# Half of the first MLP matmul moved beside the attention of the last two token groups, in an adaLN block on one core

## Chip, cores, metric

The kernel runs on one core of a Trainium2 chip. The metric is the device time of one execution in microseconds (us), as the median of several runs.

## The reference

The block works on x of 2048 tokens by 512 features, with modulation vectors from a small conditioning vector c, sliding-window attention and a token-mixing MLP.

```python
mod = (_silu(c) @ w_mod).reshape(c.shape[0], 6, 1, -1)
sa, ca, ga, sb, cb, gb = ...
h = _layernorm(x) * (1 + ca) + sa
x = x + ga * _A_ref(h, A_wqkv, A_wo)       # 32 heads of 16, window of 256 keys, causal
h = _layernorm(x) * (1 + cb) + sb
x = x + gb * _B_ref(h, ...)                # mixes over tokens:
#   h = layernorm(x)                                      (2048, 512)
#   u = gelu(einsum('bsd,sf->bdf', h, w1) + b1)           w1: (2048, 1792)
#   y = einsum('bdf,fs->bds', u, w2) + b2                 w2: (1792, 2048)
```

The contraction of the first MLP matmul runs over all 2048 tokens. Its result can be finished only when the last token's attention is done, but the part of the sum over the early tokens can be formed before.

## The kernel before, in words

Tokens are held as 16 tiles of 128 (xres, names x_65 to x_80 in the trace). Attention works on four groups G of 512 tokens, each in four units of eight heads (g8), each unit in five steps (four in group 0) that take one row of CHUNKS. A step has three parts: the score matmuls (emit_scores, L390) into two PSUM tiles of the pool ps_s, the exponential and the masks (emit_exp_mask, ScalarE L404, VectorE L411 and L416), and the matmuls with V and with ones (emit_av, L435). The scores of step i+1 are written ahead of the values of step i-1, so that ScalarE has work; ps_s has two buffers and a step needs both. After a unit emit_norm divides (L446 to L448).

Beside the steps of group G a list bg of background jobs is worked off at an even rate (per_step, L513): proj_work(G+1), which is the layer norm, transposes (L269), and Q, K, V projections (L285, L294, L313) of the next group, and post_work(G-1), which is the output projection of the group before (L344), its residual (L348), and two layer norms (L350 to L367) that end in the tiles hb (hb_81 to hb_96), the operand of the MLP. K is copied (L299) and then spread by GpSimd into a zero-padded form (L301). The padded V tiles are zeroed by three GpSimd memsets at the start (L452). Within what the code order and the buffers allow, a scheduler of the framework sets the final order on each engine.

After group 3 stands post_work(3) alone (L531), then the first MLP matmul. It takes 16 token tiles (sc) times 14 column blocks (fc) of w1, 224 matmuls of 128 by 512. Six column blocks accumulate side by side (L562), the other eight follow one by one (L570). The first half of w1, w1a, is loaded during group 1, the second half, w1b, and w2 (L539, L543) only when the attention's pools are released (att.close, L533), all on SyncE's (SP) queue. The GELU (L554) reads PSUM, VectorE scales (L557), and the second MLP matmul (L578, 224 matmuls) writes output tiles that VectorE finishes (L583, L588).

All first loads are on SP's queue as well, in the order c, x of group 0, w_mod, w_qkv, the rest. The first exponential needs x, its layer norm (xn, L245), the modulation (ps_fm L188, modFM L194), the transposes, Q and K.

## Time and profile before

| quantity | value |
|---|---|
| time, median of 3 runs (lowest to highest) | 326.96 us (326.34 to 328.46) |
| time of the profiled execution | 324.87 us |
| its span from first to last instruction | 323.2 us |
| outside the span | 1.67 us |
| TensorE (PE) matmul busy | 274.4 us, 85% |
| VectorE (DVE) busy | 209.4 us, 65% |
| ScalarE (ACT) busy | 182.3 us, 56% |
| GpSimd (POOL) busy | 39.2 us, 12% |

Busy times are sums of instruction durations over the span. Matmuls are pipelined, so that a matmul's duration is longer than the distance between two of them, and PE's busy share is above its real load. The stages of this kernel have different limits, so that shares over the span say little; the windows below cut it into stages. The granted TensorE clock is given as a share of full speed.

### The profile page before, as it was taken

How to read it: one execution, taken by the hardware profiler on the slowest of the kernel's cores; microseconds unless marked ns; L12 is line 12 of the kernel's file. 1: busy time of each engine (PE TensorE's matmuls, PEld its weight loads, DVE VectorE, ACT ScalarE, POOL GpSimd, SP SyncE). 2: the span in 40 equal slices, each digit the busy share in tenths (PEclk: the TensorE clock that was granted, in tenths of full speed). 3: DMA queues.
4: the chain of work that ended last, by engine and by line, in shares of the span. 5: the costliest groups of instructions: out<-in, count | busy, mean ns of one | idle time of the engine just before them, and what ended most of it. 6: DMA issues, size and time to landing. Idle time of an engine off the chain costs nothing.

```text
span 323.2 us, 7621 instructions
## 1 busy us (share of the span) xinstructions
PE 274.4 (85%) x3277; PEld 133.9 (41%) x3313; DVE 209.4 (65%) x487; ACT 182.3 (56%) x241; POOL 39.2 (12%) x57
## 2 busy tenths in 40 slices
PE   0388988989897889998888878968999999999994
PEld 0343435544454344454344443423334444444441
DVE  6889997758989847889846787369403112445443
ACT  2005789899996999988999999930007111000000
POOL 9632302230100230010050000000000000000000
PEclk9999999999998999979999997679999999999998
DMA  6994039000000000000000000000399910111110
GB/s 205 350 210 148 2 106 350 5 3 2 3 2 0 2 2 2 2 3 2 3 2 2 2 2 2 2 1 2 116 380 411 408 50 0 51 45 38 49 49 34
DMA packets 18121, 24.61 MB, mean 76 GB/s; under 512 B 5032, under 2 KB 14248, under 8 KB 18088
## 3 DMA queue, kind: packets, MB, share of 16 engines
q1 hardware_dynamic: 18088, 24.13, 21.7%
q8 instruction: 26, 0.43, 0.6%
q14 instruction: 7, 0.06, 0.1%
HBM read 22.03 MB, written 2.10 MB: 75 GB/s over the span
## 4 chain that ended last, share of the span: by engine, by line
PE 43%; DVE 24%; ACT 23%; issue 6%; DMA 2%; SPq 0%
ACT et L404 17%; PE py L578 15%; PE pu L570 8%; PE pss L390 5%; DVE st L237 4%; PE pox L435 3%; DVE VT_147 L323 3%; DVE xn L245 3%; PE pu L562 2%; PE pv L313 2%; PE pa L344 2%; ACT lz L446 2%; PE poy L435 2%; ACT lz L447 2%; DMA w1b<-in_B_w_dram 2%
## 5 line engine op out<-in xcount | busy, mean ns | idle before, releaser
L404 ACT ACTIVATE et<-pss 128x1024 bf16<-128x1024 f32 (+1 forms) x152 | 147.0, 1024 | 21.6 <-PE pss L390 20.8
L435 PE MATMUL poy<-et,ones_bd 128*32 128x128 bf16 (+4 forms) x768 | 43.1, 263 | 0.2
L411 DVE TENSOR_TENSOR et<-et,maskt 128x256 bf16<-128x256 bf16 (+2 forms) x104 | 33.4, 344 | 12.1 <-ACT et L404 11.8
L578 PEld LDWEIGHTS <-w2r 128*128 128x128 bf16 x224 | 21.9, 98 | 26.4
L416 DVE TENSOR_TENSOR et<-et,maskt 128x512 bf16<-128x512 bf16 x48 | 20.5, 427 | 13.5 <-ACT et L404 12.7
L435 PE MATMUL pox<-et,VT_147 128*32 128x320 bf16 (+4 forms) x352 | 20.2, 263 | 3.7 <-DVE OT_1_155 L448 1.5
L435 PEld LDWEIGHTS <-ones_bd 128*32 128x32 bf16 x768 | 19.6, 99 | 7.1 <-issue 3.6
L554 ACT ACTIVATE g<-pu,b1FM 128x512 bf16<-128x512 f32 x14 | 8.9, 696 | 16.2 <-PE pu L570 16.2
L240 ACT ACTIVATE rs<-mv,eps_t 128x4 f32<-128x4 f32 x12 | 3.6, 298 | 20.4 <-DVE mv L238 20.3
L435 PEld LDWEIGHTS <-VT_147 128*32 128x32 bf16 x352 | 9.1, 96 | 13.8 <-issue 12.9
L299 DVE CAST kb<-pk 128x512 bf16<-128x512 f32 x16 | 11.0, 687 | 4.8 <-PE pk L294 4.7
L435 PE MATMUL pox<-et,VT_148 128*32 128x320 bf16 (+4 forms) x208 | 11.0, 261 | 1.1 <-DVE OT_1_151 L448 0.6
L323 DVE CAST VT_147<-pv 64x512 bf16<-64x512 f32 x16 | 11.0, 689 | 0.8 <-PE pv L313 0.5
L435 PE MATMUL pox<-et,VT_149 128*32 128x320 bf16 (+4 forms) x208 | 11.2, 262 | 0.0
L557 DVE TENSOR_TENSOR guT_4330<-g,bc_gb 128x512 bf16<-128x512 bf16 x1 | 0.4, 424 | 16.1 <-ACT g L554 16.1
L313 PE MATMUL pv<-wqkv,h1T_159 128*64 128x256 bf16 x128 | 10.7, 294 | 0.0
L447 ACT ACTIVATE lz<-lz 128x512 f32<-128x512 f32 x16 | 10.5, 658 | 0.0
L446 ACT ACTIVATE lz<-poy 128x512 f32<-128x512 f32 x16 | 9.8, 613 | 1.1 <-PE poy L435 1.1
L294 PE MATMUL pk<-h1T_158,wqkv 128*128 128x512 bf16 x32 | 9.4, 410 | 0.7 <-DVE kb L299 0.6
L554 ACT ACT_TABLE_LOAD x1 | 1.3, 1283 | 15.5 <-PE pu L562 15.5
L285 PE MATMUL pq<-h1T_158,wqkv 128*128 128x512 bf16 x26 | 8.3, 408 | 1.6 <-issue 0.6
L570 PEld LDWEIGHTS <-w1b 128*128 128x128 bf16 x64 | 6.3, 98 | 7.6
(360 smaller groups left out, 574.7 us busy)
## 6 DMA issues: line engine op xcount, KB each, us to landing
w2r<-in_B_w_dram SPq DMA_DIRECT2D x14, 512.0 KB, 10.1
w1a<-in_B_w_dram SPq DMA_DIRECT2D x8, 448.0 KB, 7.9
...
```

What stands on the lines that cost most here:

```text
L237: nc.vector.bn_stats(out=st[:], in_=t[:])
L313: nc.tensor.matmul(pv[KB * par : KB * (par + 1), i, :].rearrange("p (a d) -> p a d", d=DH), lhsT=h1T[r2][:, dc, tok], rhs=wv[:, dc, par, : ...
L323: nc.vector.tensor_copy(out=dst, in_=src)
L390: nc.tensor.matmul(pss[:, jj, col : col + KB * nq], lhsT=KT[r][g8][rows, kbi, :, :], rhs=QT[G % 2][g8][rows, KB * qs : KB * (qs + nq)], st ...
L404: nc.scalar.activation(out=et[:, 2 * a : 2 * a + 2, lo:D], in_=tiles[a][:, :, lo:D], func=ACT.Exp, scale=SCORE_SCALE,)
L411: nc.vector.tensor_tensor(out=dst, in0=dst, in1=msk.to_broadcast([P, 4, KB * mn]), op=ALU.mult,)
L416: nc.vector.tensor_tensor(out=dst, in0=dst, in1=maskt[:, m0 : m0 + 2, :].unsqueeze(1).to_broadcast([P, 4, 2, KB]), op=ALU.mult,)
L435: nc.tensor.matmul(dst[32 * j : 32 * j + 32, KB * qs : KB * (qs + nq)], lhsT=VT[r][:, kbi, 4 * u.g8 + j, :] if isv else ones_bd[:], rhs=et ...
L446: nc.scalar.activation(out=lz[:], in_=u.y[:], func=ACT.Ln)
L447: nc.scalar.activation(out=lz[:], in_=lz[:], func=ACT.Exp, scale=-1.0)
L570: nc.tensor.matmul(pu[:], lhsT=w1s(sc, fc), rhs=hb[sc][:], start=(sc == 0), stop=(sc == NT - 1),)
L578: nc.tensor.matmul(py[:], lhsT=w2r[:, fc, tb * P : (tb + 1) * P], rhs=guT[fc][:], start=(fc == 0), stop=(fc == NF - 1),)
```

## The change

1. partial(fc) forms the sum over the first eight token tiles (1024 tokens) for one column block, eight matmuls into a ps_d buffer, and VectorE copies it to SBUF in fp32. Four of these jobs are appended to bg in group 2, ten in group 3. 112 of the 224 matmuls of the first MLP matmul thus stand among the attention steps.
2. w1 is loaded by pairs of column blocks, eight token tiles at a time (load_w1): the seven first halves at the start of group 1, each second half when the pair's two partials are formed.
3. After group 3 only the second eight token tiles are multiplied (mlp1), and before the GELU VectorE adds the partial sum. The PSUM pools stay those of the attention, so that tiles of two banks (kind s) hold two column blocks.
4. The loads of c and of the first two parts of w_mod go to ACT's queue, the w_qkv loads are split so that the columns of the first unit come first, and b1 and b2 come last.
5. V's first tile is zeroed by VectorE, the other two by 16 GpSimd memsets (zero_jobs), and group 0's first K tile is spread by VectorE straight from PSUM (no copy, no GpSimd).
6. Buffers: one h1T instead of two, h2 4 instead of 5, kb 2 instead of 3. Background jobs start a step later (credit) and are spread over one step less (nsteps - 2).

```diff
-    dma.dma_start(out=c4[:], in_=c.rearrange("o (j p) -> (o j) p", p=P))
+    nc.scalar.dma_start(out=c4[:], in_=c.rearrange("o (j p) -> (o j) p", p=P))
+    for v in (0, 1):
+        nc.scalar.dma_start(out=wmod[:, :, v * D : (v + 1) * D], in_=wm_v[:, :, v * D : (v + 1) * D])
     for t in range(4):
         dma.dma_start(out=xres[t][:], in_=x_dram[t * P : (t + 1) * P, :])
     for v in (0, 1):
-        dma.dma_start(out=wmod[:, :, v * D : (v + 1) * D], in_=wm_v[:, :, v * D : (v + 1) * D])
-    for v in (0, 1, 2):
-        dma.dma_start(out=wqkv[:, :, v * D : (v + 1) * D], in_=w_v[:, :, v * D : (v + 1) * D])
+        dma.dma_start(out=wqkv[:, :, v * D : v * D + P], in_=w_v[:, :, v * D : v * D + P])
+    dma.dma_start(out=wqkv[:, :, 2 * D : 3 * D], in_=w_v[:, :, 2 * D : 3 * D])
+    for v in (0, 1):
+        dma.dma_start(out=wqkv[:, :, v * D + P : (v + 1) * D], in_=w_v[:, :, v * D + P : (v + 1) * D])
...
+            if G == 0 and g8 == 0:
+                for par in range(2):
+                    nc.vector.tensor_scalar(
+                        out=KT[r3][g8][:, :, par, :], in0=pk[:].rearrange("p (b k) -> p b k", k=KB),
+                        scalar1=mask_par[:, par : par + 1], scalar2=0.0, op0=ALU.mult, op1=ALU.add,
+                    )
+                return
...
+    def load_w1(pair, half):
+        t = w1pool.tile([P, 8, 2 * P], BF, name=f"w1p{pair}", tag=f"w1p{pair}")
+        dma.dma_start(out=t[:], in_=w1_v[:, 8 * half : 8 * half + 8, 2 * P * pair : 2 * P * (pair + 1)])
+        w1t[pair, half] = t
...
+    def partial(fc):
+        pu = ps_d.tile([P, D], F32, name="pu", tag="psd")
+        for sc in range(8):
+            nc.tensor.matmul(
+                pu[:], lhsT=w1s(sc, fc), rhs=hb[sc][:], start=(sc == 0), stop=(sc == 7),
+            )
+        pool = partA if fc < 4 else partB
+        t = pool.tile([P, D], F32, name=f"part{fc}")
+        nc.vector.tensor_copy(out=t[:], in_=pu[:])
+        part[fc] = t
+        if fc % 2 == 1:
+            load_w1(fc // 2, 1)
...
-    for r in range(3):
-        nc.gpsimd.memset(VT[r][:], 0.0)
+    nc.vector.memset(VT[0][:], 0.0)
...
+    zero_jobs = [lambda r=r, kb=kb: zero_v(r, kb) for r in (1, 2) for kb in range(8)]
...
-            post = post_work(u.G - 1) if u.G > 0 else mod_jobs + [early, wod_scale]
+            post = post_work(u.G - 1) if u.G > 0 else mod_jobs + [early, wod_scale] + zero_jobs[8:]
...
+            if u.G == 0:
+                bg = zero_jobs[:8] + bg
+            if u.G == 2:
+                bg += [lambda fc=fc: partial(fc) for fc in range(4)]
+            if u.G == 3:
+                bg += [lambda fc=fc: partial(fc) for fc in range(4, NF)]
             nsteps = sum(1 for s in steps if s[0].G == u.G)
-            per_step = len(bg) / (nsteps - 1)
-            credit = 0.0
+            per_step = len(bg) / (nsteps - 2)
+            credit = -per_step
...
+    f_tiles([("s", [0, 1]), ("s", [2, 3]), ("x", [4]), ("y", [5])])
+    for w in pw:
         w()
+    mlp1(first, range(8, NT))
     att.close()
...
-    w1b = w2pool.tile([P, 8, F], BF, name="w1b")
-    for sc in range(8):
-        dma.dma_start(out=w1b[:, sc, :], in_=w1_v[:, 8 + sc, :])
...
+    def gelu(fc):
+        a = gtmp.tile([P, D], F32, name="a")
+        nc.vector.tensor_tensor(out=a[:], in0=ftiles[fc], in1=part[fc][:], op=ALU.add)
         g = gtmp.tile([P, D], BF, name="g")
         nc.scalar.activation(
-            out=g[:], in_=pu[:], func=ACT.Gelu_apprx_tanh, bias=b1FM[:, fc : fc + 1], scale=1.0,
+            out=g[:], in_=a[:], func=ACT.Gelu_apprx_tanh, bias=b1FM[:, fc : fc + 1], scale=1.0,
         )
```

The order on the engines changes at three places. On GpSimd, near the start, the kernel before zeroes the three V tiles (VT_147 to VT_149) between the identity and the masks:

```order
masks.py:197 MEMSET identity 128x128
L117 MEMSET ones_bd 128x32
L452 MEMSET VT_147 128x4096
masks.py:199 ISA
masks.py:199 AFFINE_SELECT identity<-identity 128x128
L118 MEMSET ones_bd 64x16
L119 MEMSET ones_bd 64x16
L452 MEMSET VT_148 128x4096
L452 MEMSET VT_149 128x4096
```

Now the masks come first, and the 16 short memsets of two V tiles (VT_144, VT_145) follow in one run ahead of the K tiles:

```order
L234 COPY maskt<-tmpm 64x64
L235 COPY maskt<-tmpm 64x64
L503 MEMSET VT_144 128x512 x8
L503 MEMSET VT_145 128x512 x8
L314 TENSOR_SCALAR KT_1_132<-kb,mask_par 128x8x64 x2
L314 TENSOR_SCALAR KT_2_133<-kb,mask_par 128x8x64 x2
```

What moved: three long memsets became sixteen short ones behind the masks, and none of the sixteen waits for another engine. On DVE the copy of the first half of modFM now stands ahead of the four normalisations xn of group 0, where it stood behind them.

On TensorE, in the last unit of group 3, the scores (pss) are followed at once by the matmuls with V (pox) and ones (poy) in the kernel before:

```order
L390 MATMUL pss<-QT_3_134,KT_3_146 128x256
L390 LDWEIGHTS KT_3_146
L390 MATMUL pss<-QT_3_134,KT_3_146 128x256
L435 LDWEIGHTS VT_147
L435 MATMUL pox<-et,VT_147 32x192
```

Now the eight matmuls of a partial sum (pu, weights w1p) stand between the two (three of the eight are shown):

```order
L403 LDWEIGHTS KT_3_142
L403 MATMUL pss<-QT_3_130,KT_3_142 128x256
L446 LDWEIGHTS w1p_1249
L446 MATMUL pu<-hb_81,w1p_1249 128x512
L446 LDWEIGHTS w1p_1249
L446 MATMUL pu<-hb_82,w1p_1249 128x512
L446 LDWEIGHTS w1p_1249
L446 MATMUL pu<-hb_83,w1p_1249 128x512
```

What moved: every step from the end of the second unit of group 3 on carries about one such run of eight, the last carries two, and the end of group 2 carries 2 and 14 and 16 matmuls in three places.

On TensorE, behind the last step of attention, the output projection (pa) is followed in the kernel before by the first MLP matmul over the first token tile (hb_81, w1a):

```order
L344 MATMUL pa<-wod,OT_2_156 128x512
L344 LDWEIGHTS OT_3_157
L344 MATMUL pa<-wod,OT_3_157 128x512
L562 LDWEIGHTS w1a
L562 MATMUL pu<-hb_81,w1a 128x512
```

Now part of the output projection is done ahead of the last unit's OT_3, and the matmuls that follow are of the second half of the tokens (hb_89 is the ninth tile):

```order
L357 LDWEIGHTS OT_1_151
L357 MATMUL pa<-wod,OT_1_151 128x512
L357 LDWEIGHTS OT_2_152
L357 MATMUL pa<-wod,OT_2_152 128x512
L596 LDWEIGHTS w1p_3283
L596 MATMUL pu_4409<-hb_89,w1p_3283 128x512
```

What moved: the 61 matmuls over the first half of the tokens that stood here in front of the first one that reads hb_89 are gone. Now 32 matmuls over hb_89 to hb_92 stand in front of the first one that reads hb_93, and 80 from there to the end of the first MLP matmul. Of the second MLP matmul's first tile five stand ahead of the last block of those.

## Rows read from the trace of the kernel before

**Rows 1.** Windows: stretch, length, busy us (instructions) PE, PEld, DVE, ACT, POOL; clock, DMA, GB/s.

```profile
0.00:24.00 24.00, 9.62 (x110) 6.34 (x111) 18.95 (x37) 2.69 (x5) 15.46 (x27) 1.00 0.90 254
76.50:124.50 48.00, 41.77 (x729) 21.73 (x727) 37.74 (x97) 42.84 (x55) 6.42 (x8) 0.96 0.01 2
...
182.00:192.60 10.60, 8.37 (x164) 4.30 (x161) 8.49 (x25) 10.54 (x15) 0.00 (x0) 1.00 0.01 3
192.60:212.40 19.80, 17.17 (x287) 8.06 (x288) 11.87 (x35) 17.73 (x24) 0.00 (x0) 0.74 0.01 2
...
229.40:270.00 40.60, 39.02 (x177) 17.32 (x180) 6.50 (x16) 9.45 (x14) 0.00 (x0) 1.00 0.70 272
```

**Rows 2.** Timeline behind the last step of group 3: start, duration, engine, line.

```profile
212.37 0.60 ACT L446 ACTIVATE lz<-poy 128x512 f32<-128x512 f32 x1 [1.09 <-PE poy L435]
...
214.41 0.89 PE L344 MATMUL pa<-wod,OT_3_157 128*128 128x512 bf16 x2 [2.09 <-DVE OT_3_157 L448]
...
217.32 0.63 PE L344 MATMUL pa<-wod,OT_0_154 128*128 128x512 bf16 x1
...
218.31 0.38 PE L344 MATMUL pa<-wod,OT_3_157 128*128 128x512 bf16 x1
...
228.99 0.41 DVE L245 TENSOR_SCALAR hb_93<-h_4258,mv,rs 128x512 bf16<-128x512 bf16 x1 [0.60 <-ACT rs L241]
...
230.51 4.26 SPq L539 DMA_DIRECT2D w1b<-in_B_w_dram  x8
```

**Rows 3.** Chain that ended last, in order of time: start, us, what.

```profile
257.14 10.74 PE pu L570 x49
...
318.42 0.76 DVE o_4945 L583
```

**Rows 4.** Page, part 5, groups by line: busy us, mean ns, then idle before.

```profile
L554 ACT ACTIVATE g<-pu,b1FM 128x512 bf16<-128x512 f32 x14 | 8.9, 696 | 16.2 <-PE pu L570 16.2
...
L299 DVE CAST kb<-pk 128x512 bf16<-128x512 f32 x16 | 11.0, 687 | 4.8 <-PE pk L294 4.7
...
L557 DVE TENSOR_TENSOR guT_4330<-g,bc_gb 128x512 bf16<-128x512 bf16 x1 | 0.4, 424 | 16.1 <-ACT g L554 16.1
...
L554 ACT ACT_TABLE_LOAD x1 | 1.3, 1283 | 15.5 <-PE pu L562 15.5
```

**Rows 5.** Page, part 2: DMA rate in 40 slices of 8.1 us.

```profile
GB/s 205 350 210 148 2 106 350 5 3 2 3 2 0 2 2 2 2 3 2 3 2 2 2 2 2 2 1 2 116 380 411 408 50 0 51 45 38 49 49 34
```

**Rows 6.** Timeline of PE at the end of group 1.

```profile
117.36 0.27 PE L435 MATMUL pox<-et,VT_148 128*32 128x192 bf16 x4
...
117.92 0.41 PE L390 MATMUL pss<-QT_0_127,KT_0_139 32*128 32x192 bf16 x12
```

**Rows 7.** Timeline of the first 30 us.

```profile
3.06 0.98 SPq L151 DMA_DIRECT2D wmod<-in_w_mod_dram  x2
...
5.11 3.52 POOL L452 MEMSET VT_148<- 128x4096 bf16 x1
...
7.59 0.10 PEld L188 LDWEIGHTS <-wmod 128*128 128x128 bf16 x1 [1.07 <-DMA wmod<-in_w_mod_dram]
...
8.45 3.77 DVE L245 TENSOR_SCALAR xn<-x_65,mv,rs 128x512 bf16<-128x512 bf16 x1 [0.60 <-ACT rs L241]
8.56 3.52 POOL L452 MEMSET VT_149<- 128x4096 bf16 x1
...
12.02 0.46 POOL L215 MEMSET tmpm<- 128x256 bf16 x1
...
13.64 0.99 PE L188 MATMUL ps_fm<-sT,wmod 128*128 128x1 bf16 x32 [7.03 <-DVE sT L178]
...
24.05 0.81 ACT L404 ACTIVATE et<-pss 128x768 bf16<-128x768 f32 x1 [4.87 <-PE pss L390]
...
29.50 0.70 POOL L301 TENSOR_SCALAR KT_1_136<-kb,mask_par 128x512 bf16<-128x512 bf16 x1 [5.40 <-DVE kb L299]
29.55 0.79 DVE L245 TENSOR_SCALAR xn<-x_70,mv,rs 128x512 bf16<-128x512 bf16 x1
```

More of the change, by code (lines that the diff above doesn't have):

```diff
@@ L130 @@
     OT = [[kvpool.tile([P, D], BF, name=f"OT{r}_{g}") for g in range(ND)] for r in range(2)]
-    h1T = [kvpool.tile([P, ND, D], BF, name=f"h1T{r}") for r in range(2)]
     work = att.enter_context(tc.tile_pool(name="work", bufs=3))
     epool = att.enter_context(tc.tile_pool(name="epool", bufs=6))
-    ps_d = att.enter_context(tc.tile_pool(name="ps_d", bufs=2, space=PSUM))
-    ps_s = att.enter_context(tc.tile_pool(name="ps_s", bufs=2, space=PSUM))
-    ps_o = att.enter_context(tc.tile_pool(name="ps_o", bufs=1, space=PSUM))
+    wpool = tc.alloc_tile_pool(name="wpool", bufs=1)
+    wqkv = wpool.tile([P, ND, 3 * D], BF, name="wqkv")
+    w_v = A_wqkv.rearrange("(j p) n -> p j n", p=P)
+    h1T = wpool.tile([P, ND, D], BF, name="h1T")
+    ps_d = ctx.enter_context(tc.tile_pool(name="ps_d", bufs=2, space=PSUM))
+    ps_s = ctx.enter_context(tc.tile_pool(name="ps_s", bufs=2, space=PSUM))
+    ps_o = ctx.enter_context(tc.tile_pool(name="ps_o", bufs=1, space=PSUM))
     w1_v = B_w1.rearrange("(sc p) f -> p sc f", p=P)
+    w1t = {}
+    part = {}
     modw = tc.alloc_tile_pool(name="modw", bufs=1, side="right")
@@ L258, in ln1 @@
             for i in range(4):
[L259 removed]
+                t = wpool.tile([P, D], BF, name="xn", tag="xn", bufs=5)
                 normalize(t[:], xres[4 * G + i][:], mv, rs, i)
@@ L274, in tr @@
                 nc.vector.tensor_scalar(
-                    out=h1T[r2][:, dc, :], in0=pt[:, i, :],
+                    out=h1T[:, dc, :], in0=pt[:, i, :],
                     scalar1=modFM[:, 4 + dc : 5 + dc], scalar2=modFM[:, dc : dc + 1],
@@ L496 @@
                 w1pool = ctx.enter_context(tc.tile_pool(name="w1pool", bufs=1, side="right"))
-                w1a = w1pool.tile([P, 8, F], BF, name="w1a")
-                for sc in range(8):
-                    dma.dma_start(out=w1a[:, sc, :], in_=w1_v[:, sc, :])
+                partA = ctx.enter_context(tc.tile_pool(name="partA", bufs=1, side="right"))
+                for pair in range(NF // 2):
+                    load_w1(pair, 0)
+            if u.G == 3:
+                wpool.release()
+                partB = ctx.enter_context(tc.tile_pool(name="partB", bufs=1, side="right"))
             done_group = u.G
             bg = []
-            post = post_work(u.G - 1) if u.G > 0 else mod_jobs + [early, wod_scale]
+            post = post_work(u.G - 1) if u.G > 0 else mod_jobs + [early, wod_scale] + zero_jobs[8:]
             proj = proj_work(u.G + 1) if u.G + 1 < NG else []
@@ L530, with f_tiles, mlp1 @@
         w()
-    for w in post_work(NG - 1):
+    ftiles = {}
+    def f_tiles(fcs):
+        for kind, group in fcs:
+            if kind == "s":
+                t = ps_s.tile([P, 2, D], F32, name="pu2", tag="pss")
+                for i, fc in enumerate(group):
+                    ftiles[fc] = t[:, i, :]
+            else:
+                pool, tag = {"x": (ps_o, "pox"), "y": (ps_o, "poy"), "d": (ps_d, "psd")}[kind]
+                t = pool.tile([P, D], F32, name="pu1", tag=tag)
+                ftiles[group[0]] = t[:]
+    def mlp1(fcs, scs):
+        for sc in scs:
+            for fc in fcs:
+                nc.tensor.matmul(
+                    ftiles[fc], lhsT=w1s(sc, fc), rhs=hb[sc][:], start=(sc == 8), stop=(sc == NT - 1),
+                    skip_group_check=True,
+                )
+    pw = post_work(NG - 1)
+    first = list(range(6))
+    f_tiles([("s", [0, 1]), ("s", [2, 3]), ("x", [4]), ("y", [5])])
+    for w in pw:
         w()
+    mlp1(first, range(8, NT))
     att.close()
     w2pool = ctx.enter_context(tc.tile_pool(name="w2pool", bufs=1))
-    w1b = w2pool.tile([P, 8, F], BF, name="w1b")
-    for sc in range(8):
-        dma.dma_start(out=w1b[:, sc, :], in_=w1_v[:, 8 + sc, :])
     w2r = w2pool.tile([P, NF, S], BF, name="w2r")
@@ L589 @@
         dma.dma_start(out=out_dram[tb * P : (tb + 1) * P, :], in_=ot[:])
+    homes = [("d", 1), ("d", 1), ("s", 2), ("s", 2), ("x", 1), ("y", 1)]
+    tb = 0
+    i = 0
+    while tb < NT:
+        kind, n = homes[i % len(homes)]
+        i += 1
+        f_tiles([(kind, list(range(100 + tb, 100 + tb + n)))])
+        for t in range(tb, tb + n):
+            for fc in range(NF):
+                nc.tensor.matmul(
+                    ftiles[100 + t], lhsT=w2r[:, fc, t * P : (t + 1) * P], rhs=guT[fc][:],
+                    start=(fc == 0), stop=(fc == NF - 1), skip_group_check=True,
+                )
+            finish(t, ftiles[100 + t])
+        tb += n
 _INS = ['A_x', 'A_wqkv', 'A_wo', 'B_x', 'B_w1', 'B_b1', 'B_w2', 'B_b2', 'c', 'w_mod']
```

60 lines of the change are left out of this document (21 added, 39 removed).

## The prediction

> **What bounds the kernel now.** I read the windows by stage first, because the shares over the whole span mix limits; then the timeline at the stages' borders, and the chain. In the first 24 us PE works 9.6 us and DVE 19.0 [rows 1]: VectorE and the loads lead to the first exponential, which starts at 24.05 [rows 7]. Group 1 takes 48.0 us with ACT busy 42.8. Group 3 has no projections: its second unit takes 10.6 us with ACT busy 10.5, so there ScalarE is the bound, at 2.1 us a step, and over the next 19.8 us the granted clock of PE is 0.74 because PE has room. From 229.4 on PE is the bound, 39.0 of 40.6 us [rows 1], and all of the chain's time [rows 3]. Between, from 212.4 to 229.4, lies the chain of VectorE from the last attention output to the last four hb tiles. PE fills it with the first half of the MLP matmul.
>
> The change takes 112 matmuls from the stage that PE bounds to stages that ScalarE bounds. What it earns is the tail's shortening less what groups 2 and 3 grow.
>
> **The tail.** Let T be the start of the last unit's logarithm, 212.37 [rows 2]. Before, hb_93 starts at T+16.6 and the span ends at T+110.8. After: the order puts 32 MLP matmuls and the output projection in front of hb_93, and 80 behind it. The pitch of a matmul follows from the chain: a piece of 49 takes 10.74 us [rows 3]; a matmul lasts 0.38 [rows 2], so the last one's overhang is some 0.16, and 10.58/49 is 0.216. So
> - hb_93 starts at T+16: the chain is the same, and the output projection is some tenths earlier, because three of its four parts stand ahead of OT_3;
> - 80 matmuls of 0.216: 17.3;
> - lower clock at the start: 16 matmuls of output projection and 32 of the MLP are 10 us of PE in a gap of 16, so PE rests some 4 us ahead of hb_93. Before, after a rest of 2.1 us, PE restarted at 214.41, and a matmul at 217.32 still took 0.63 us, one at 218.31 then 0.38 [rows 2]: some 3.4 us at the lower clock. Half of that is lost: 1.7;
> - 224 matmuls: 48.4; the wait for the last GELUs: 0.6 (below); from the last matmul to the end as before, 323.2 less 318.42 [rows 3]: 4.8.
>
> That is T+88.8, 22.0 us earlier against T. The new additions on VectorE run beside PE: 14 times 0.69 (the K copy reads the same PSUM shape) and 14 scalings of 0.42 are 15.5 us, and the GELU table load 1.3 [rows 4], from about T+20.5 on. They end at T+37.5, and the second MLP matmul needs the last guT at about T+39. The w2 load waits for the release behind hb_96, as w1b did at 230.51 [rows 2], T+18.1. 7.3 MB at the 380 to 411 GB/s of the slices [rows 5] are 18 to 19 us, so it lands at about T+38, just in time; at the 272 GB/s of the whole window [rows 1], which holds idle time, it would be T+45 and cost 5. Range of this term: -18 to -24.
>
> **Groups 2 and 3.** A step's attention matmuls need S on PE. The lower bound: 16 of the 24 value matmuls stand between 117.36 and 117.92, 0.56 us, and the 12 score matmuls behind them take 0.41 [rows 6], hence 1.0. The upper bound: group 1 has 48.0 us for 20 steps and some 15 us of projections (32 matmuls of Q and K and 16 of the output at 0.216, V and transposes by their columns 4.5), hence (48.0 - 15)/20 = 1.65. I take 1.3, the first with all 24 value matmuls (0.28 more). In group 3 the ten partial sums stand in the last 12 steps by the order. Before, these took 24.0 us (19.8 and two of 2.1 [rows 1]). After, PE needs 80 times 0.216 and 12 times 1.3, 32.9: +8.9 (+5.3 to +13.2). ScalarE cannot work ahead, since a step takes both score buffers. In group 2 four sums stand in the last three steps: 6.9 + 3.9 = 10.8 against 7.2 at group 1's 2.4 a step: +3.6 (+2.7 to +4.7). VectorE copies 14 sums of 0.69, 9.7 us, in stretches where it works 60 to 80%. A mask behind a copy waits up to 0.69; I take 1.5 for that and for the jobs spread over fewer steps (0 to 3). Together +14, from +8 to +21. That PE is no longer at ease also keeps its clock up; the lower clock hurt little before, since ScalarE led.
>
> **The start.** Before, the first xn (layer norm of group 0) starts at 8.45 and takes 3.77 us; it ends as the memset of VT_149 does, and the next takes 0.47 [rows 7]; the fourth ends at about 13.3. After: c and w_mod no longer queue behind x. w_mod's first part, issued at 3.06 before, can start at about 1.3; its weights loaded at 7.59 before, 4.5 behind the issue [rows 7], so modFM's first half is there at about 6.4, no later than the statistics of x. DVE's work from x's landing to xn is about 4.7 us (four statistics of some 0.8 with their sums, small ones for silu and sT), hence xn from 7.6 on. The sixteen memsets run in this time. GpSimd's other work takes until about 4.4 (15.46 busy [rows 1] less three of 3.52 and two of 0.70 for K, from 0.9 on). One memset of 512 takes between 0.44 (an eighth of 3.52) and 0.66 (between 0.46 for 256 and 3.52 for 4096 [rows 7]), so the run ends at 11.4 to 15. If VectorE gets in between two of them, four xn of 0.33 end at 9 to 11, say 10, against 13.3. Behind that, ps_fm's 0.99 is already done (-1.1) and K needs no copy and no GpSimd (-0.4, as V still stands between): the first exponential comes at 10 + 9.3 = 19.3, 4.8 us earlier. If VectorE has to wait for the whole run, xn ends at 12.7 to 16.3, and the gain is +2 to a loss of 1.5.
>
> Which? Row against row: xn_65 waited out a memset that ran already and lost to VT_149's, which started 0.11 later; xn_70 at 29.55 took 0.79 beside two GpSimd instructions for K of 0.70 each [rows 7], which is one instruction's wait and then its own work. The second case, with short instructions, is nearer, so I take -5 (+1.5 to -6).
>
> By the Trainium skill, page "SBUF — State Buffer", section "Who interferes with whom", the port pair that VectorE and GpSimd share is an exclusive lock, held for the whole instruction by whoever comes first. By that rule each xn would lose at most one short memset, and the sum would stand. The row of xn_65 does not agree: it also lost the border to the next memset.
>
> Sum: -5 + 14 - 22 = -13. On the profiled execution (324.87, of which 1.67 outside the span) this is 311.9; the median of the runs shown is 2.1 above the profiled one, hence 314.
>
> At nothing I cost the w1 loads by pairs (DMA idles at 0.01 beside attention [rows 1]; without that cover the last pair's second half, issued at about T, would be late for the last two blocks only), the single h1T (its readers are done a group earlier), and b1 and b2 at the end of the queue (VectorE copies them at about the sixth step; if they landed later, the masks would stand behind them, 1 to 3 us).
>
> **The rivals.**
> 1. GpSimd's run of memsets holds VectorE to its end. For it: xn_65's row. Against it: xn_70's. Start 0 instead of -5: 319.
> 2. The GELU chain becomes the bound of the tail: if VectorE and ScalarE take turns for each block (0.69 + 0.70 + 0.42 [rows 4], 25 us for 14, and 1.3 for the table), it ends at T+47 and the second matmul starts 7 us late. Against it: the scheduler sets several additions ahead of the first scaling. 321.
> 3. Slower than before: the partial sums run at the lower clock. Group 3's second half had 0.74. At half speed the 80 matmuls take 34.2 instead of 17.3 us and the attention's 12 steps about 3.7 more: 20.6 more, 335. It decides where this loss passes 13 us, with some three quarters of that stretch's time at half speed, a mean clock of about 0.6. Against it: in group 1, where PE has projections to do, the clock is 0.96 [rows 1], and the sums add as much.
>
> **How the numbers follow.** I give my forecast 0.57, the memset rival 0.2, the GELU chain 0.13, the low clock 0.08, other things 0.02. A measurement of this kernel can tell about 1% (3.3 us) from no change. The forecast and most of rivals 1 and 2 are faster by more than that: 0.83; parts of rivals 1 and 2 give the 0.08 within 1%; the low clock and the rest 0.09. The terms' ends added up give -22 to +4.5, 305 to 331; both ends need all terms at their worst or best. Left out above 323 is the low clock and the worst of the others, about a tenth, below 306 less than a tenth; so the range is 306 to 323.
>
> **What would show it.** In the profile after: the first exponential at about 19; in group 3 a length of 50 to 51 instead of 41.5, ScalarE idle before its exponentials with PE (L403) as what ended it; a clock near 1.00 there; from the last logarithm to the end 89 us, with 0.6 of waits between the two MLP matmuls. Wrong it would be if PE in group 3 still waited for ScalarE (then S is small and the gain larger), if xn again showed a duration of microseconds, if the second MLP matmul waited for guT or w2r, or if the partial sums' matmuls stood 0.43 apart.

## The result and the profile after

The changed kernel takes 317.76 us (median of 4 runs, 316.47 to 318.46) against 326.65 us for the kernel before on the same chip (4 runs, 324.27 to 328.46), a ratio of 0.9728, 95% interval 0.9657 to 0.9798. It is faster, by 8.9 us between the medians and by 6.9 us between the two profiled runs (spans 323.2 and 316.3, on which the working below stands). The prediction was 314, from 306 to 323.

One table holds the stages of every kernel of this study. Its borders are read from the timelines: the first exponential, and the start of each unit's logarithm (L446 before, L480 after), the fourth of which ends a group. The first two columns are points of time, the next ones lengths; span and stages are of one profiled run, the median is of all runs. The tail runs from the last logarithm to the end of the span. The median of e6 leaves out one slow run (316.43).

| kernel | first exp. | end of group 0 | group 1 | group 2 | group 3 | tail | span | median |
|---|---|---|---|---|---|---|---|---|
| before | 24.05 | 72.56 | 49.4 | 49.7 | 40.7 | 110.8 | 323.2 | 326.65 |
| after | 23.33 | 72.59 | 50.9 | 56.6 | 48.4 | 87.8 | 316.3 | 317.76 |
| e1_zero_by_dma | 23.31 | 73.22 | 50.8 | 56.6 | 48.3 | 88.0 | 316.9 | 318.61 |
| e5_loads | 23.55 | 72.50 | 50.9 | 56.7 | 48.4 | 88.0 | 316.5 | 318.52 |
| e9_x_late | 21.41 | 72.59 | 49.9 | 56.3 | 48.4 | 89.5 | 316.7 | 318.24 |
| e12_double | 29.96 | 79.24 | 50.7 | 56.5 | 48.4 | 87.8 | 322.5 | 324.16 |
| e2_spacing | 22.99 | 72.78 | 49.9 | 56.7 | 48.4 | 87.9 | 315.6 | 318.74 |
| e8_before_dense | 23.44 | 72.69 | 50.8 | 50.9 | 43.2 | 110.8 | 328.4 | 330.75 |
| e4_spread | 24.79 | 74.06 | 49.9 | 56.3 | 49.6 | 88.7 | 318.6 | 320.06 |
| e3_gap4 | 23.69 | 72.95 | 50.9 | 50.9 | 48.3 | 88.5 | 311.6 | 313.72 |
| e6_gap_spacing | 24.17 | 73.97 | 49.7 | 49.5 | 50.4 | 88.5 | 312.1 | 314.20 |
| e7_all | 22.76 | 72.22 | 49.4 | 49.5 | 50.7 | 88.7 | 310.6 | 312.98 |
| e11_best_old_start | 22.14 | 71.93 | 49.4 | 50.0 | 48.3 | 88.5 | 308.2 | 310.05 |
| e10_best | 20.57 | 70.94 | 49.4 | 50.1 | 48.4 | 88.8 | 307.6 | 309.54 |

From before to after: 0.0 at the end of group 0, +1.5 in group 1, +6.9 in group 2, +7.7 in group 3, -23.0 in the tail. A difference of 1 us in one stage of two profiles is no evidence by itself: e4 has the code of the changed kernel up to group 2, and yet its first exponential is 1.5 us later and its group 1 is 1.0 shorter.

The windows of the changed kernel by stage, with the columns of [rows 1], show where PE became the bound:

```profile
95.64:111.93 16.29, 11.62 (x195) 6.55 (x193) 13.79 (x35) 11.32 (x17) 0.00 (x0) 0.79 0.01 2
...
146.85:164.17 17.32, 13.49 (x198) 6.29 (x195) 13.69 (x35) 12.62 (x19) 2.17 (x3) 0.80 0.01 2
164.17:180.13 15.96, 14.38 (x194) 6.62 (x190) 7.56 (x16) 10.45 (x14) 2.55 (x4) 1.00 0.24 68
180.13:192.07 11.94, 10.35 (x169) 4.80 (x173) 9.05 (x23) 11.01 (x16) 0.00 (x0) 1.00 0.01 1
192.07:202.63 10.56, 9.22 (x162) 4.78 (x163) 10.53 (x32) 10.37 (x15) 0.00 (x0) 1.00 0.01 2
202.63:216.95 14.32, 13.77 (x196) 6.26 (x198) 8.20 (x21) 10.73 (x15) 0.00 (x0) 1.00 0.27 76
216.95:228.49 11.54, 10.83 (x163) 5.27 (x158) 5.87 (x14) 6.81 (x8) 0.00 (x0) 1.00 0.36 98
```

and the longest wait of ScalarE over the last two (engine, line, what it waited for: us, times, longest):

```profile
ACT et L417 <- PE pss L403: 4.8, 5, 1.5
```

The last four rows are group 3's units. Its second unit still takes 10.6 us with ACT busy all the time, as in [rows 1]. The two units with the partial sums grew to 14.3 and 11.5 (11.2 and 8.5 before) with PE busy nearly throughout and the granted clock at 1.00 instead of about 0.74; ScalarE waits 4.8 us there for PE's scores, where it waited 0.8 before. The first unit grew as well, from 10.3 to 11.9, although hardly a matmul of a sum stands in it. In group 2 the fourth unit (164.17 on) holds four sums and is PE's as well. But the third units of groups 1 and 2 (the first two rows) are long for another reason: PE is busy 11.6 and 13.5 us of 16.3 and 17.3, VectorE almost 14, the clock is 0.8, and in group 1 there is no partial sum at all.

The tail on PE's timeline (start, duration, instruction, idle time before it):

```profile
238.60 0.38 PE L596 MATMUL pu_4623<-hb_92,w1p_4073 128*128 128x512 bf16 x1
244.66 1.01 PE L596 MATMUL pu_4409<-hb_93,w1p_3283 128*128 128x512 bf16 x2 [5.67 <-DVE hb_93 L251]
245.46 0.63 PE L596 MATMUL pu_4410<-hb_93,w1p_3350 128*128 128x512 bf16 x1
...
247.81 0.59 PE L596 MATMUL pu_4410<-hb_94,w1p_3350 128*128 128x512 bf16 x2
248.24 0.38 PE L596 MATMUL pu_4411<-hb_94,w1p_3965 128*128 128x512 bf16 x1
...
261.63 0.38 PE L653 MATMUL pu_4719<-guT_4562,w2r 128*128 128x512 bf16 x1
```

PE runs out of work at 239.0 and rests 5.67 us for hb_93. Then a matmul takes 0.63 us until about 247.8, the half-clock duration that [rows 2] shows after the shorter rest of the kernel before. The second MLP matmul starts at 261.63, T+33.1 with T = 228.49.

The start, on VectorE's timeline:

```profile
8.43 0.16 DVE L244 BATCH_NORM_AGGREGATE mv<-st 128x2 f32<-128x6 f32 x1
8.54 3.62 DVE L186 COPY sT_rep<-sT 128x512 bf16<-128x512 bf16 x1
12.08 0.14 DVE L200 COPY modFM<-ps_fm 128x4 f32<-128x4 f32 x1
12.15 0.40 DVE L251 TENSOR_SCALAR xn<-x_65,mv,rs 128x512 bf16<-128x512 bf16 x1
...
14.05 0.69 DVE L243 BATCH_NORM_STATS2 st<-x_69 128x6 f32<-128x512 bf16 x1 [0.47 <-DMA x_69<-in_A_x_dram]
14.66 1.89 DVE L280 TENSOR_SCALAR h1T<-pt,modFM 128x512 bf16<-128x512 bf16 x4
```

and on GpSimd's the two times eight memsets:

```profile
4.29 3.86 POOL L503 MEMSET VT_144<- 128x512 bf16 x8
8.10 3.78 POOL L503 MEMSET VT_145<- 128x512 bf16 x8
```

The copy sT_rep (the silu of c, spread out as an operand of matmuls), 0.43 us in the kernel before, takes 3.62 and ends 0.28 us after the run of memsets does (11.88). So xn starts at 12.15, not at 7.6, and the first exponential moved by 0.7 us only.

### The profile page after: what moved, and what is told of

The parts are those of the page before. It is cut to its first block, busy times and chain, and to the rows that moved or that the text cites. A ratio compares the mean times of both kernels' runs of the same rounds, so it can differ in the third digit from the quotient of the medians.

```text
span 316.3 us, 7673 instructions
## 1 busy us (share of the span) xinstructions
PE 266.9 (84%) x3271; PEld 130.4 (41%) x3313; DVE 229.4 (73%) x517; ACT 184.2 (58%) x241; POOL 33.8 (11%) x68
## 4 chain that ended last, share of the span: by engine, by line
PE 45%; ACT 20%; DVE 19%; issue 5%; another core or an unknown queue 0%
ACT et L417 15%; PE pu L446 6%; PE pss L403 5%; DVE st L243 4%; PE pox L469 4%; PE poy L469 2%; ACT lz L481 2%; PE pu_4759 L653 2%; PE pu_4917 L653 2%; PE pu_4798 L653 2%; PE pu_4956 L653 2%; PE pq L291 2%; PE pv L326 2%; DVE et L424 2%; ACT lz L480 1%
## 5 line engine op out<-in xcount | busy, mean ns | idle before, releaser
L417 ACT ACTIVATE et<-pss 128x1024 bf16<-128x1024 f32 (+1 forms) x152 | 146.8, 1022 | 33.3 <-PE pss L403 32.9
L469 PE MATMUL poy<-et,ones_bd 128*32 128x128 bf16 (+4 forms) x768 | 42.4, 257 | 2.6 <-DVE et L424 2.4
L424 DVE TENSOR_TENSOR et<-et,maskt 128x256 bf16<-128x256 bf16 (+2 forms) x104 | 35.4, 360 | 12.3 <-ACT et L417 12.0
L429 DVE TENSOR_TENSOR et<-et,maskt 128x512 bf16<-128x512 bf16 x48 | 21.2, 442 | 18.0 <-ACT et L417 17.4
L469 PE MATMUL pox<-et,VT_143 128*32 128x320 bf16 (+4 forms) x352 | 19.4, 259 | 3.5 <-DVE OT_1_151 L482 1.2
L291 PE MATMUL pq<-h1T,wqkv 128*128 128x512 bf16 x58 | 17.1, 401 | 3.0 <-DVE VT_143 L336 1.3
L326 PE MATMUL pv<-wqkv,h1T 128*64 128x256 bf16 x256 | 18.6, 285 | 0.6 <-DVE KT_0_131 L306 0.5
L300 PE MATMUL pk<-h1T,wqkv 128*128 128x512 bf16 x57 | 16.5, 397 | 2.2 <-DVE kb L312 0.9
L621 ACT ACTIVATE g<-a,b1FM 128x512 bf16<-128x512 f32 x14 | 9.6, 716 | 12.4 <-DVE a L619 12.4
L326 PEld LDWEIGHTS <-h1T 128*64 128x64 bf16 x256 | 13.3, 113 | 4.7 <-issue 2.6
L469 PEld LDWEIGHTS <-VT_143 128*32 128x32 bf16 x352 | 9.1, 96 | 13.5 <-issue 12.9
L312 DVE CAST kb<-pk 128x512 bf16<-128x512 f32 x15 | 10.3, 688 | 5.6 <-issue 2.5
L469 PE MATMUL pox<-et,VT_144 128*32 128x320 bf16 (+4 forms) x208 | 11.1, 268 | 2.5 <-DVE OT_1_147 L482 2.1
L480 ACT ACTIVATE lz<-poy 128x512 f32<-128x512 f32 x16 | 9.7, 608 | 4.4 <-PE poy L469 4.3
L469 PE MATMUL pox<-et,VT_145 128*32 128x320 bf16 (+4 forms) x208 | 11.1, 261 | 1.0 <-DVE OT_2_152 L482 0.5
L300 PEld LDWEIGHTS <-wqkv 128*128 128x128 bf16 x64 | 5.5, 101 | 9.5 <-issue 4.7
L291 PEld LDWEIGHTS <-wqkv 128*128 128x128 bf16 x64 | 5.5, 100 | 8.5 <-issue 3.6
```

The lines of the kernel that those rows point to most:

```text
L291: nc.tensor.matmul(pq[:], lhsT=wqkv[:, dc, g8 * P : (g8 + 1) * P], rhs=h1T[:, dc, :], start=(dc == 0), stop=(dc == ND - 1),)
L300: nc.tensor.matmul(pk[:], lhsT=wqkv[:, dc, D + g8 * P : D + (g8 + 1) * P], rhs=h1T[:, dc, :], start=(dc == 0), stop=(dc == ND - 1),)
L326: nc.tensor.matmul(pv[KB * par : KB * (par + 1), i, :].rearrange("p (a d) -> p a d", d=DH), lhsT=h1T[:, dc, tok], rhs=wv[:, dc, par, :, :] ...
L417: nc.scalar.activation(out=et[:, 2 * a : 2 * a + 2, lo:D], in_=tiles[a][:, :, lo:D], func=ACT.Exp, scale=SCORE_SCALE,)
L424: nc.vector.tensor_tensor(out=dst, in0=dst, in1=msk.to_broadcast([P, 4, KB * mn]), op=ALU.mult,)
L429: nc.vector.tensor_tensor(out=dst, in0=dst, in1=maskt[:, m0 : m0 + 2, :].unsqueeze(1).to_broadcast([P, 4, 2, KB]), op=ALU.mult,)
```

## Experiments on the start

**e1_zero_by_dma** takes the run of memsets away: V's second and third tile are zeroed by late DMAs.

```diff
+    nc.vector.memset(zeros[:], 0.0)
...
+    for r in (1, 2):
+        dma.dma_start(
+            out=VT[r][:].rearrange("p b h d -> p b (h d)"), in_=zeros[:].unsqueeze(1).to_broadcast([P, 8, DH * 2 * DH]),
+        )
...
-        nc.gpsimd.memset(VT[r][:, kb, :, :], 0.0)
...
+    zero_jobs = [lambda: None] * 16
```

> Edit: the 16 GpSimd memsets at the start are gone; V's second and third tile are zeroed by two DMAs from a small tile of zeros, late on SP's queue. Theory A (the run of memsets held VectorE to its end): sT_rep takes some 0.4 us instead of 3.62, the first exponential starts 3 to 4 us earlier, at 19.5 to 20.5 instead of 23.33, and since VectorE bounds the first unit (busy 27.9 of 29.3 us behind the first exponential), the whole of VectorE's work moves with it: time 3 to 4 us less, about 314. Rival B (sT_rep waits for something else, or the loads): first exponential stays at 23 +- 0.5, time within 1 us. Rival C: first exponential at 20, but the end of group 0 stays at about 83.8, because a load or VectorE's queue of group 0 takes the gain back: time within 1 us.

VectorE's timeline of e1:

```profile
8.66 0.39 DVE L186 COPY sT_rep<-sT 128x512 bf16<-128x512 bf16 x1
9.97 0.16 DVE L200 COPY modFM<-ps_fm 128x4 f32<-128x4 f32 x1 [0.92 <-PE ps_fm L194]
10.05 1.37 DVE L251 TENSOR_SCALAR xn<-x,mv,rs 128x512 bf16<-128x512 bf16 x4
...
13.86 0.69 DVE L243 BATCH_NORM_STATS2 st<-x 128x6 f32<-128x512 bf16 x1 [2.37 <-DMA x<-in_A_x_dram]
14.47 1.88 DVE L280 TENSOR_SCALAR h1T<-pt,modFM 128x512 bf16<-128x512 bf16 x4
```

The copy takes 0.39 us and xn comes 2.1 us earlier, so theory A is right about the memsets. But the first exponential stays at 23.31, and the time (318.61) within 1 us. (The 83.8 that the expectation calls the end of group 0 is the end of group 1's first unit; the end of group 0 is 72.59 in the changed kernel and 73.22 here.) The statistics of x_69, a tile of the next group, stand ahead of h1T in VectorE's order, and that tile's load lands at about 14 in both kernels. In the changed kernel the same wait shows with 0.47 us and is easy to overlook, since the memsets covered most of it.

**e12_double** issues each memset twice.

```diff
-    zero_jobs = [lambda r=r, kb=kb: zero_v(r, kb) for r in (1, 2) for kb in range(8)]
+    def zero_twice(r, kb):
+        zero_v(r, kb)
+        zero_v(r, kb)
+
+    zero_jobs = [lambda r=r, kb=kb: zero_twice(r, kb) for r in (1, 2) for kb in range(8)]
```

> Edit: the changed kernel with each of the 16 GpSimd memsets issued twice, so that the run of GpSimd is 7.7 us longer (16 times 0.48) and ends at about 19.5; VectorE's order at the start is the same. Theory A (VectorE's copy waits until the run has an end): sT_rep takes 11 us instead of 3.62, from 8.5 to 19.5, and the first exponential comes 7 to 8 us later, at 31. Rival B (VectorE gets in between two memsets after some time, as the rule of a lock held for one instruction has it): sT_rep stays below 4 us, first exponential at 23 to 25.

VectorE's timeline of e12:

```profile
5.86 0.94 DVE L178 RECIPROCAL rm<-em 4x128 f32<-4x128 f32 x1
...
7.57 0.65 DVE L243 BATCH_NORM_STATS2 st<-x 128x6 f32<-128x512 bf16 x1
...
8.56 11.08 DVE L186 COPY sT_rep<-sT 128x512 bf16<-128x512 bf16 x1
```

Theory A: the copy takes 11.08 us and the first exponential comes at 29.96, 6.6 us later than in the changed kernel (7 to 8 were expected). The delay goes through to the end: group 0 ends 6.6 us later, and the one run took 324.16 us, 6.4 more. The statistics at 7.57 took their usual 0.65 us within the same run of GpSimd.

**e5_loads** and **e9_x_late** both keep e1's edit (no GpSimd memsets) and go for the second wait, by the place of x_69 to x_72 in SP's queue: e5 puts them ahead of w_qkv's rest, e9 behind the four other parts of w_mod (and both put b1 and b2 ahead of wod). The edit of e9, and then that of e5:

```diff
-    for t in range(4, 8):
-        dma.dma_start(out=xres[t][:], in_=x_dram[t * P : (t + 1) * P, :])
     for v in (2, 4, 3, 5):
         dma.dma_start(out=wmod[:, :, v * D : (v + 1) * D], in_=wm_v[:, :, v * D : (v + 1) * D])
+    for t in range(4, 8):
+        dma.dma_start(out=xres[t][:], in_=x_dram[t * P : (t + 1) * P, :])
```

```diff
+    for t in range(4, 8):
+        dma.dma_start(out=xres[t][:], in_=x_dram[t * P : (t + 1) * P, :])
     for v in (0, 1):
         dma.dma_start(out=wqkv[:, :, v * D + P : (v + 1) * D], in_=w_v[:, :, v * D + P : (v + 1) * D])
-    for t in range(4, 8):
-        dma.dma_start(out=xres[t][:], in_=x_dram[t * P : (t + 1) * P, :])
```

> Edit: as e1_zero_by_dma (no GpSimd memsets), and the loads of x_69 to x_72 go ahead of the rest of w_qkv, b1 and b2 ahead of wod. In e1 xn came 2.1 us earlier, but VectorE's next work was the statistics of x_69, which stood ahead of h1T in its order and waited 2.37 us for that tile's load (start 13.86). Theory A (the start is a row of two waits of equal end, the run of memsets and this load, and both must go): h1T starts at about 12, the first exponential at 20.5 to 21.5 instead of 23.3, and the time is 2 to 3 us below e1's 318.6. Rival B (a third thing ends at the same time, w_qkv's first part or K): first exponential at 23 +- 0.5, time as e1 within 1 us. Rival C: first exponential at 21 but the end of group 0 within 1 us of e1's 73.2: VectorE's queue of group 0 holds other loads (x_73 to x_80) and gives it back.

> Edit: as e1_zero_by_dma (no GpSimd memsets), and the loads of x_69 to x_72 go behind the four parts of w_mod, so that the statistics of x_69 stand behind h1T and the first K tile in VectorE's order; b1 and b2 go ahead of wod. In e5, where that load was earlier, the statistics moved to before xn and VectorE waited 3.67 us for it there. Theory A (it is this wait, wherever it stands, that ends the start): h1T starts at 11.8 to 12.5 instead of 14.5, first exponential at 20.5 to 21.5, and as VectorE is busy all of group 0's first unit, the end of group 0 moves from 72.6 to 71 or less: time 1.5 to 2.5 us below the changed kernel's, 315 to 316. Rival B: first exponential at 21, but the end of group 0 stays within 0.7 us of 72.6, since the statistics only moved from the start into the first unit, where VectorE has no idle time: time within 1 us.

In e5 the scheduler answered the earlier load by moving the statistics ahead of sT_rep and xn, where VectorE waited 3.67 us for x_69 (landed at 11.9): first exponential 23.55, time 318.52, rival B's number by a cause of its own. In e9 the statistics stand behind the first K tile; h1T starts at 12.55 and the first exponential at 21.41. Group 0 ends at 72.59 all the same, to the hundredth where it did (rival B; 318.24 us). The first unit's window of e9, a part of it, and VectorE's longest wait in it

```profile
21.41:39.54 18.13, 16.06 (x166) 6.61 (x170) 16.78 (x44) 13.38 (x18) 4.36 (x6) 0.85 0.70 204
...
35.41:37.41 2.00, 2.00 (x15) 0.38 (x10) 1.98 (x9) 1.38 (x3) 0.00 (x0) 0.50 0.00 0
...
38.55 0.69 DVE L211 TENSOR_SCALAR bc_ga<-ps_b 128x512 bf16<-128x512 f32 x1 [1.17 <-PE ps_b L206]
```

and of the changed kernel

```profile
23.33:40.19 16.86, 14.37 (x164) 6.29 (x167) 16.59 (x44) 12.77 (x19) 4.42 (x6) 1.00 0.21 25
```

show VectorE busy for 16.8 and 16.6 us, so it bounds this unit in the changed kernel. Of the 1.9 us that e9 gains at the first exponential, 0.65 are left at the end of the first unit, 0.3 after the second, nothing after the third. Two things can have taken them, and no run separates the two. The four statistics of 0.66 us that e9 moves behind the first exponential are work for VectorE there, and later statistics move on to the next units. But the granted clock is also 0.50 from about 34.5 to 41, where it was 1.00 in the changed kernel, and VectorE waits 1.17 us for a product of PE there. Rival B's time thus came; its reason is argued, not shown.

## Experiments on the spacing of the jobs

**e2_spacing** undoes the last edit alone.

```diff
-            per_step = len(bg) / (nsteps - 2)
-            credit = -per_step
+            per_step = len(bg) / (nsteps - 1)
+            credit = 0.0
```

> Edit: the background jobs are spread as before (over nsteps - 1 steps, beginning at once). Theory A (the denser jobs put VectorE's layer-norm work and the casts in a pile, so that a unit's last multiplication is late, PE rests over 2 us and then runs for some 6 us at half clock): the third units of groups 1 and 2, 16.3 and 17.3 us, come back to 13 to 14, and the time falls by 4 to 6 us. Rival B (the smaller buffers, one h1T, or the partial sums themselves are to blame): both units stay above 16, time within 1 us.

Group 1's third unit fell from 16.3 to 13.2, as theory A has it, but the group as a whole only by 1.0 us, since its other units grew; group 2's third unit fell only from 17.3 to 16.9, and the time (318.74) stayed within 1 us, against theory A. **e8_before_dense** makes the same edit the other way round, in the kernel before, which has neither partial sums nor smaller buffers.

```diff
-            per_step = len(bg) / (nsteps - 1)
-            credit = 0.0
+            per_step = len(bg) / (nsteps - 2)
+            credit = -per_step
```

> Edit: the kernel before, with only the changed spacing of the background jobs (over nsteps - 2 steps, a step later). Theory A (the denser jobs alone make the third units of groups 1 and 2 longer, by a late last multiplication and half clock behind it): these grow from 14.0 and 13.0 to 16, time 2 to 4 us above before. Rival B (it takes the single h1T or the smaller buffers too): units within 1 us of before, time within 1 us.

Theory A: 330.75 us, 1.0104 of before (1.0055 to 1.0154), a small loss but clear of none; the third units of groups 1 and 2 grow from 14.0 and 13.0 to 16.2 and 16.3, the groups by 1.4 and 1.2, and group 3 by 2.5 us too. The table agrees: group 1 takes 49.9 to 50.9 us in the eight kernels with the changed spacing, 49.4 to 49.9 in the six with the old one there. Windows of 2 us in the third unit of group 1 of e8 show how:

```profile
95.70:97.70 2.00, 2.00 (x40) 1.22 (x35) 2.00 (x7) 2.00 (x5) 0.00 (x0) 1.00 0.04 8
97.70:99.70 2.00, 0.11 (x2) 0.09 (x1) 1.92 (x4) 1.87 (x3) 0.00 (x0) 1.00 0.00 0
99.70:101.70 2.00, 0.40 (x3) 0.19 (x3) 1.97 (x6) 0.00 (x0) 0.00 (x0) 0.75 0.00 0
101.70:103.70 2.00, 1.93 (x39) 0.88 (x41) 1.96 (x7) 0.90 (x1) 0.00 (x0) 0.50 0.00 0
103.70:105.70 2.00, 2.00 (x28) 1.48 (x27) 1.97 (x7) 1.51 (x3) 0.00 (x0) 0.50 0.00 0
105.70:107.70 2.00, 2.00 (x34) 0.95 (x31) 1.36 (x3) 0.95 (x3) 0.00 (x0) 0.54 0.04 8
```

and the waits in that unit (columns as above):

```profile
ACT et L404 <- PE pss L390: 4.8, 3, 3.2
...
PE poy L435 <- DVE et L411: 2.4, 1, 2.4
PE pox L435 <- DVE OT L448: 1.2, 1, 1.2
```

VectorE is busy throughout with a pile of layer-norm jobs, so that a mask and the division of the unit before are late; PE does 0.5 us of work in 4, and then runs at half clock (0.50) for 6 us although it is busy again. In the changed kernel the same windows of this unit, taken from 95.64 on, are the same within 0.1 us of busy time and 0.04 of the clock.

## Experiments on the partial sums

**e3_gap4** leaves the four column blocks of group 2 whole for the tail, so that 32 matmuls lie in PE's rest ahead of hb_93, straight into the PSUM tiles in which they end. These four blocks then need no copy and no addition before the GELU, and both halves of their w1 are loaded in group 1.

```diff
+    NH = 4
...
-            if u.G == 2:
-                bg += [lambda fc=fc: partial(fc) for fc in range(4)]
...
+    mlp1(range(NH), range(8))
     mlp1(first, range(8, NT))
...
```

> Edit: no partial sums in group 2; the four column blocks they belonged to are summed whole behind the attention, their first half (32 matmuls) into the PSUM tiles in which they end, without copy or addition. Theory A (PE's rest of 5.67 us ahead of hb_93 and the lower clock behind it are free room, and the sums cost their full PE time in group 2): the fourth unit of group 2 falls from 16.0 to 12.1 (-3.9), the tail behind the last logarithm gains 32 matmuls of 0.216 (6.9 us) but loses 5.67 us of rest and 1.7 of low clock, -0.5: time 4 to 5 us less, about 313. Rival B (the 32 matmuls come in the way of the output projection and of the chain that leads to hb_93): the tail is 4 to 7 us longer, time 0 to 3 us more.

Theory A: 313.72 us. Group 2 falls from 56.6 to 50.9, of which the fourth unit from 16.0 to 11.6; the tail grows by 0.7. In e3 PE rests 0.49 us ahead of hb_93, and the clock there is 1.00.

**e4_spread** lets the ten sums of group 3 alternate with the layer-norm jobs from its start.

```diff
-                bg += [lambda fc=fc: partial(fc) for fc in range(4, NF)]
+                jobs = [lambda fc=fc: partial(fc) for fc in range(4, NF)]
+                bg = [w for pair in zip(jobs, bg) for w in pair]
```

> Edit: in group 3 the ten partial sums alternate with the ten jobs of the output projection and layer norms from the group's start, instead of standing behind them. Theory A (PE is the bound only where the sums stand; ScalarE bounds the first units): PE needs 20 steps of 1.3, 80 + 16 matmuls of 0.216, 46.7 us, against the 48.4 measured: 1 to 2 us less, and the two last units even out. Rival B (VectorE, busy 10.5 of 10.6 us in the second unit, cannot take five more copies of 0.69 there): the second unit grows from 10.6 to 13 or more, the last layer norms of the group's jobs come later, time 1 to 4 us more.

320.06 us and a second unit of 13.7 are rival B's numbers, but not its cause. The windows of e4 for the four units of group 3:

```profile
180.30:193.77 13.47, 12.73 (x188) 5.73 (x190) 9.01 (x21) 10.65 (x14) 0.00 (x0) 1.00 0.15 40
193.77:207.47 13.70, 12.61 (x193) 5.68 (x189) 9.37 (x25) 11.00 (x14) 0.00 (x0) 1.00 0.14 39
207.47:220.93 13.46, 9.38 (x174) 4.74 (x171) 11.80 (x34) 10.86 (x15) 0.00 (x0) 1.00 0.25 67
220.93:229.91 8.98, 7.66 (x142) 4.25 (x144) 4.44 (x11) 6.72 (x10) 0.00 (x0) 1.00 0.09 26
```

In the first two units PE is busy 12.7 of 13.5 and 12.6 of 13.7 us, VectorE only 9; the layer norms that were put off fill VectorE in the third; and in the last, where PE had room, it is busy for only 7.7 us: five or six of the ten sums stand in the first two units, two in each of the others. Group 3 is 1.2 us longer than in the changed kernel. The rest of the 2.3 us cannot be put down to this edit: the first exponential is 1.5 us later and groups 1 and 2 are 1.3 shorter, where the code is the same, and the tail is 0.9 longer.

**e6_gap_spacing**, **e7_all**, **e10_best** and **e11_best_old_start** put the parts together. e6 is e2 and e3; e7 is e6 with e5; e10 takes e9, e3, and the old spacing in groups 0 to 2 only; e11 is e10 with the start of the changed kernel. The edit of e10 and e11 to the spacing:

```diff
-            per_step = len(bg) / (nsteps - 2)
-            credit = -per_step
+            late = 1 if u.G == 3 else 0
+            per_step = len(bg) / (nsteps - 1 - late)
+            credit = -per_step * late
```

> Edit: e3_gap4 (no partial sums in group 2, four blocks whole behind the attention) and e2_spacing (jobs spread as before) together. In e2 the third unit of group 1 fell from 16.3 to 13.2, that of group 2, which still had the sums among its jobs, only from 17.3 to 16.9. Theory A (the number of jobs a step decides, 1.21 as before): third units of groups 1 and 2 at 13 to 13.5 both, group 2 at 49.7 as before the change instead of 50.9, time 2 us below e3's 313.7. Rival B (the single h1T holds group 2's projections): group 2's third unit stays at 16, time as e3.

> Edit: e5_loads, e2_spacing and e3_gap4 in one kernel. If the three terms are independent, the time is e3's 313.7 less 2 for the spacing and less 2 to 3 for the start: 309 to 310. If group 0 or VectorE's queue takes the start's gain back: 312.

> Edit: e9_x_late, e3_gap4, and the old spacing of the jobs in groups 0 to 2 with the changed one in group 3 only. In e6 and e7 groups 1 and 2 came back to 49.4 to 49.7 us, but group 3, whose partial sums then began a step earlier beside VectorE's layer norms, grew from 48.3 to 50.4 and 50.7. Theory A (each group has its own bound): groups 1 and 2 at 49.5, group 3 at 48.3, tail 88.5, time 2 us below e7's 312.98 and 1 to 2 more for the start: 309 to 311. Rival B (group 3's length hangs on something else that differs between e3 and e6): group 3 stays above 50, time 312 to 313.

> Edit: as e10_best, but with the start of the changed kernel (16 GpSimd memsets, its order of loads). The start's worth in the best kernel is the difference to e10's 309.5. Theory A (with the old spacing the gain of 2 to 3 us at the first exponential carries through to the end): first exponential at 23 to 24, end of group 0 at 72.6 to 74, time 311.5 to 312.5. Rival B (group 0 takes it back here too, as in e9): time 309 to 310.

In e6 the third units are 14.2 and 13.9, groups 1 and 2 as long as before the change; it is the number of jobs a step, not the single h1T. But group 3 grows to 50.4, and the time (314.20) is e3's. e7 (312.98, where 309 to 310 was expected of independent terms) repeats this. The growth is in the second unit. Its windows in e6 and in e2, which has the same jobs and the same spacing in group 3:

```profile
184.98:197.61 12.63, 11.74 (x164) 5.06 (x163) 10.60 (x32) 10.55 (x15) 0.00 (x0) 0.74 0.01 1
...
191.14:201.79 10.65, 9.45 (x163) 4.72 (x163) 10.47 (x32) 10.53 (x15) 0.00 (x0) 1.00 0.01 2
```

VectorE and ScalarE have the same work in both, and the sums begin 11.4 us into the group in both (10.9 in the changed kernel); in e6 the granted clock is 0.50 from the unit's start for about 6 us. So an earlier start of the sums, as e10's expectation has it, does not explain the growth. What lowers the clock in e6 and e7 and not in e2 stays open.

With the late spacing kept in group 3 alone, that group is back at 48.3 and 48.4 with the clock at 1.00, and e11 takes 310.05 us (0.9475 of before, 0.9412 to 0.9539), e10 309.54 (0.9477, 0.9411 to 0.9543; its runs of before had a median of 327.82). Both lie clearly below the changed kernel's interval. From e11 to e10 the start is worth 1.6 us at the first exponential, 1.0 at the end of group 0 and 0.5 in the median, which these runs cannot tell from nothing. The granted clock over the 40 slices of e10's page has one dip left (in group 2's third unit, 14.6 us long), where the changed kernel had its 0.8 in two units:

```profile
PEclk9999999999999999999799999999999999999998
```

## Why the prediction was right and wrong

Its sum was -5 for the start, +14 for the groups, -22 for the tail, -13 in all. The profiled runs give 0.0 (at the end of group 0), +16.1 and -23.0, or -6.9. Of the 6.1 us between, 5.0 are the start's, 2.1 the groups', and the tail gave back 1.0.

- **The tail** was right, step by step: hb_93 at T+15.7 (T+16 predicted), some 3.2 us at the lower clock (3.4 taken), the second MLP matmul at T+33.1 with 72 matmuls in front of it, the end at T+87.8 (T+88.8). Rival 2 did not come: behind hb_93 PE waits only once more, for 0.2 us, so the GELU chain and the w2 load are no bound.
- **Group 3** grew by 7.7 where 8.9 stood, and the two are not the same thing. The prediction priced the last twelve steps. The last two units take 25.9 us; with the two steps ahead, as in the prediction's own count, 30.1 instead of 32.9, which is +6.1 against the kernel before. Less 17.3 for 80 matmuls this leaves 1.07 us of PE a step: near the lower bound (1.0), not the 1.3 taken. The other 1.6 us are in the group's first unit, which no term of the sum had. There the jobs of the group before stand denser, and ScalarE (busy 11.0 of 11.9 us) has two small instructions of their layer norm, 0.5 us, and a wait of 0.4 for VectorE's statistics; what makes up the rest was not tried. Rival 3 did not come: the clock in all four units is 1.00, as was argued.
- **Group 2**: the four sums cost 5.7 us (56.6 against e3's 50.9), where 3.6 stood and 4.7 was the upper end. 4.4 of it are in the fourth unit, where their matmuls are, 1.0 in the third. With the old spacing they cost more, 7.2 (e2 against e6).
- **"1.5 for that and for the jobs spread over fewer steps (0 to 3)"** was too small, though inside its own bounds. e8 puts the spacing alone at +3.5 us in the kernel before; from e3 to e11, where only the spacing of groups 0 to 2 differs, it is 3.7, of which 1.0 in group 0; in groups 1 and 2 of the changed kernel it is 2.7 (1.5, and e3's 50.9 less 49.7). The last is a remainder: undone alone (e2), the spacing gives back 1.0 in group 1 and nothing in group 2, as long as the sums stand among its jobs. The step priced a mask that waits for one copy of 0.69. What the runs showed is a pile of jobs, a rest of PE, and 6 us at half clock behind it. So the three terms came out at 7.7 + 5.7 + 2.7 = 16.1.
- **The start, "I take -5"**, is the step that failed. Rival 1's time, 319, is near what came, and its mechanism is what e12 shows: VectorE waits to the end of the run of memsets, with sT_rep, not xn. By the rule of the Trainium skill that the prediction quoted (page "SBUF — State Buffer", section "Who interferes with whom") a copy should lose one memset of some 0.5 us. The traces differ: it lost the 7 that were still to come, and in e12 all 23. But the rival's account was short as well: with the memsets gone (e1) nothing is gained. xn still starts at 10.05 and not at 7.6, because the copy of modFM stands ahead of it and waits for PE's product of sT, which is ready at 8.58; and the statistics of x_69 hold h1T until that load ends, as late as the memsets made it. With both waits gone the first exponential comes 1.9 us earlier in e9 than in the changed kernel, 1.6 earlier in e10 than in e11, and at the end of group 0 nothing and 1.0 us of that are left. The prediction carried an earlier first exponential to the end unreduced, and had not asked what bounds the unit after it.

The median of 317.76 is 3.8 us above the forecast of 314, inside its range. That it is not 6.1 above is chance: the prediction added 2.1 us because its profiled run lay below the median, and the profiled run after (317.99) lies 0.2 above it.
